# Six of thirty exponentials computed as powers on GpSimd, under another fixed order of all engines

## The chip, the cores and the metric

The kernel runs on one core of one Trainium2 chip. The metric is the device time of one execution in microseconds (us), lower is better. A core has TensorE (matrix products into PSUM, eight banks), VectorE (DVE in the profile), ScalarE (ACT), GpSimd (POOL) and SyncE (SP, which here only issues transfers). Each engine works through its own list of instructions in order; semaphores make it wait for others.

## The reference, cut to what matters

Two branches work on the same `A_x` of 2048 tokens by 640 columns, and a gate per token mixes them. (The second input, `B_x`, isn't used by the result.)

```python
x = A_x
g = sigmoid((x * gate_w).sum(-1, keepdims=True))
return g * A(x, wq, wk, wv, wo, beta) + (1 - g) * B(x, w_r, w_i)

def A(...):                       # 32 heads of 20, four segments of 512 tokens
    phi = lambda t: where(t > 0, t + 1.0, exp(t))
    for s in range(4):
        logits = qs @ ks^T * scale + mask     # causal within the segment
        a_dot = softmax(logits) @ vs
        a_mem = (phi(qs) @ M) / (phi(qs) @ z + 1e-06)
        outs.append(sigmoid(beta) * a_mem + (1 - sigmoid(beta)) * a_dot)
        M = M + phi(ks)^T @ vs
        z = z + phi(ks).sum(tokens)
    return concat(outs) @ wo

def B(x, w_r, w_i):               # 2-D Fourier filter
    return irfft2(rfft2(x) * (w_r + 1j * w_i))
```

`phi` is what the change touches. It is needed for `q` in segments 1 to 3 (the memory is empty in segment 0) and for `k` in segments 0 to 2 (nothing reads the memory after segment 3). Queries and keys of a segment are five tiles of 128 rows (head columns) by 512 tokens, so there are 6 x 5 = 30 tiles.

## The kernel before

The attention branch goes segment by segment. `proj_tile` (L1007) makes one tile of `q` or `k`: matmuls into a PSUM bank, a copy into SBUF (`ev_proj`, on ACT or VectorE), a store to DRAM from where the heads are read back padded (`qkp`), and then `phi` of the tile. `phi` is three instructions: `phi_exp` (L1052, on ACT) writes exp of the tile into one of two buffers `et`; `phi_max` (L1064, VectorE) writes max(t, 0) + 1 into `phq` or `phk`; `phi_min` (L1065, VectorE) takes the minimum of the two. For `k`, a transposing load `pkT` then makes `pkn`, which the memory update multiplies with `va`.

The attention itself takes head groups of four. `qk_unit` makes the logits in four PSUM banks, ACT writes their exponentials into `ex` (L1247), GpSimd zeroes what lies above the diagonal (`mask`, L1273), and `pv_flipped` (`pv_group` in the last segment) multiplies with the values. `ex` has three buffers, so a group's exponentials need the buffer that the third group before it used. `ev_pv` copies the result into `ub`. Beside all this runs the Fourier branch, as matrix products against tables: `fold` sums of rows on VectorE and GpSimd, `F1`, `D`, `T`, then the product with the filter (`W_mul` on VectorE, L1429; `W_add`, L1434, on VectorE or GpSimd), and back (`Tb`, `Db`). `finish_tile` makes the output. Reversed copies of `x` (`xrev`, L924) are made by ACT or GpSimd.

No loop sets the order. The kernel first records all 2291 operations, each with its possible engines, a cost of the planner's and its dependencies. Then `schedule` goes through a list written out in the kernel, `ORDER` (L550): each code is twice the operation's number plus the choice among its engines. Every engine gets its instructions in the order of this list, and `emit` adds the semaphore waits that the dependencies need. A second list, `HOMES` (L538), names the PSUM bank of each result. So an instruction whose input is late holds up all that the list places behind it on its engine.

Costs in the planner are a fixed part and a part per column in nanoseconds. `either` (L493), for a VectorE instruction that GpSimd can do instead, gives GpSimd 120 + 1.95 per column.

Of the kernel before, what the change touches and what calls it, by code (L numbers as in the profile page):

```python
# [417 lines left out]
SC = float(DH) ** -0.5  # L418


class Kern:
# [79 lines left out]
    def dma(self, dst, src, nbytes, r, w, prio, tr=False, name="", after=(), queue="sp"):  # L501
# [343 lines left out]
    def consts(self):  # L845
# [10 lines left out]
        for i in range(2):  # L856
            self.one("pool", lambda e, i=i: e.memset(self.va[i].ap(0, [1, 4 * H * VW + 16]), 1.0), 2816, [],
                     [b("va", i, lt, h) for lt in range(4) for h in range(2)], 0.0)
# [738 lines left out]
```

## Time and profile before

| | |
|---|---|
| three runs | 248.64, 255.21, 257.80 us |
| their median | 255.21 us |
| span of the profiled execution | 246.3 us |
| mean granted TensorE clock | 0.999 |
| instructions | 11384 |

The profile is of one execution: the span goes from its first instruction to its last. What lies around the span isn't part of it; the fastest of the three runs is 2.3 us above it. The page gives each engine's busy time and then the chain of work that ended last; the views of the trace group instructions by line and tile, and give waits as total, times and longest in us. A group's row reads: line, engine, operation, output and input tiles with their shapes, count, then busy us and mean ns of one, then idle us before them and what ended it. L484 and L482 are the PSUM copies of `copy_alts` on VectorE and ACT.

### The profile page before, as it was taken

The numbers are of one execution on the slowest core, as the hardware profiler recorded it, in microseconds if no ns is written. First come the engines' busy times: TensorE is split into PE (matmuls) and PEld (weight loads), VectorE is DVE, ScalarE is ACT, GpSimd is POOL, SyncE is SP. The second block draws the span as 40 slices with busy tenths as digits, with TensorE's granted clock in tenths as the row PEclk, the third lists the DMA queues.
The fourth block names the chain that finished last, engine by engine and source line by source line (L and its number), as shares of the span: only waits on it lengthen the run. The fifth ranks groups of instructions, "written<-read, shape, count | busy, mean of one in ns | idle before, by whom it ended". The sixth has DMA issues, their size and how long they took to land.

```text
span 246.3 us, 11384 instructions
## 1 busy us (share of the span) xinstructions
PE 223.4 (91%) x4926; PEld 145.0 (59%) x4926; DVE 193.4 (79%) x475; ACT 197.5 (80%) x231; POOL 149.9 (61%) x276
## 2 busy tenths in 40 slices
PE   6999998799799899999869997999899889999992
PEld 1576566677466466556635754546555557667891
DVE  0189897689799799799899798999989784755552
ACT  2199977879799899899878987998899959798720
POOL 8123327147656944828966984866887558567810
PEclk9999999999999999999999999999999999999999
DMA  7899779985659495669762783444866567952223
GB/s 170 263 368 189 211 216 182 296 141 164 149 156 243 143 178 153 193 175 187 212 161 65 227 233 73 141 142 157 247 183 150 140 172 181 150 122 72 68 93 96
DMA packets 58933, 42.25 MB, mean 172 GB/s; under 512 B 30020, under 2 KB 55172, under 8 KB 58884
## 3 DMA queue, kind: packets, MB, share of 16 engines
q1 hardware_dynamic: 57188, 40.71, 65.8%
q10 hardware_dynamic: 1696, 0.82, 1.3%
q8 instruction: 39, 0.64, 1.1%
q14 instruction: 10, 0.08, 0.1%
HBM read 23.32 MB, written 12.30 MB: 145 GB/s over the span
## 4 chain that ended last, share of the span: by engine, by line
PE 40%; DVE 15%; DMA 14%; ACT 12%; SPq 8%; POOL 5%; issue 3%; DVEq 0%; ACTq 0%; POOLq 0%
PE psum L473 25%; PE psum L471 15%; ACT ex L1247 11%; SPq L505 5%; SPq L507 4%; POOL ex L1273 4%; DMA fcat<-tab_fcat 3%; DMA tt<-tab_tt 2%; DMA pkn<-phk 2%; DVE Pt L1429 2%; DMA qk_scr<-qu 2%; DMA xsb<-in_A_x_dram 2%; DMA u_scr<-ub 2%; DVE phq L1064 2%; DVE Cp L484 2%
## 5 line engine op out<-in xcount | busy, mean ns | idle before, releaser
L1247 ACT ACTIVATE ex<-psum 128x2048 bf16<-128x2048 f32 (+4 forms) x92 | 137.2, 1505 | 17.6 <-PE psum L473 13.9
L1273 POOL TENSOR_SCALAR_AFFINE_SELECT ex<-ex 128x256 bf16<-128x256 bf16 (+3 forms) x191 | 93.8, 514 | 32.2 <-ACT ex L1247 27.7
L473 PE MATMUL psum<-qkp 20*64 20x64 bf16 (+5 forms) x1024 | 32.1, 266 | 5.7 <-ACT ex L1247 3.0
L1429 DVE TENSOR_TENSOR Pt<-psum,Wt 128x642 bf16<-128x642 f32 x32 | 25.8, 818 | 3.6 <-PE psum L473 2.1
L1434 POOL TENSOR_TENSOR Yt<-Pt 128x321 bf16<-128x321 bf16 x24 | 17.5, 736 | 15.5 <-DVE Pt L1429 11.9
L473 PEld LDWEIGHTS psum<-qkp 20*64 20x64 bf16 (+1 forms) x1024 | 12.4, 100 | 23.9 <-ACT ex L1247 14.1
L473 PE MATMUL psum<-xT,wk 128*128 128x256 bf16 (+1 forms) x220 | 22.4, 293 | 0.8 <-DMA xT<-in_A_x_dram 0.8
L471 PE MATMUL psum<-wo,oU 128*32 128x320 bf16 x480 | 20.4, 299 | 0.8 <-DVE oU L1524 0.8
L877 POOL TENSOR_TENSOR xsb<-xf 128x318 bf16<-128x318 bf16 (+2 forms) x9 | 7.0, 793 | 20.7 <-DVE xf L872 20.7
L473 PEld LDWEIGHTS psum<-xT,wk 128*128 128x128 bf16 (+1 forms) x220 | 14.7, 102 | 6.9 <-issue 3.6
L473 PE MATMUL psum<-ex,va 128*32 128x192 bf16 (+4 forms) x480 | 17.7, 273 | 0.8 <-DVE Cp L484 0.3
L473 PE MATMUL psum<-xT,wq 128*128 128x512 bf16 (+1 forms) x95 | 18.0, 419 | 0.0
L1475 DVE TENSOR_TENSOR G<-eo,psum 128x320 bf16<-128x320 f32 x32 | 14.0, 479 | 4.0 <-PE psum L473 3.5
L1095 DVE TENSOR_TENSOR va<-psum,ebx 128x320 bf16<-128x320 f32 x32 | 15.1, 480 | 1.6 <-ACT gate L1093 0.7
L473 PEld LDWEIGHTS psum<-ex,va 128*32 128x32 bf16 x480 | 11.8, 96 | 7.7 <-issue 1.4
L1052 ACT ACTIVATE et<-qu 128x512 bf16<-128x512 bf16 x25 | 15.6, 628 | 0.2 <-DVE phq L1065 0.2
L473 PE MATMUL psum<-wv,xT 128*128 128x320 bf16 (+2 forms) x90 | 15.3, 248 | 0.0
L471 PEld LDWEIGHTS psum<-wo,oU 128*32 128x32 bf16 x480 | 12.4, 97 | 4.5 <-DVE oU L1524 1.1
L484 DVE CAST Cp<-psum 65x256 bf16<-65x256 f32 (+1 forms) x26 | 13.6, 536 | 1.6 <-PE psum L471 1.2
L484 DVE CAST ot<-psum 128x320 bf16<-128x320 f32 x17 | 8.2, 490 | 7.5 <-PE psum L471 3.5
L872 DVE TENSOR_TENSOR xf<-xsb 128x640 bf16<-128x640 bf16 x16 | 7.3, 482 | 8.1 <-DMA xsb<-in_A_x_dram 8.1
L471 PE MATMUL psum<-xT,wq 128*32 128x512 bf16 x160 | 11.6, 380 | 2.3 <-DVE va L1095 1.3
(122 smaller groups left out, 472.9 us busy)
## 6 DMA issues: line engine op xcount, KB each, us to landing
qkp<-qk_scr SPq DMA_DIRECT2D x28, 160.0 KB
tt<-tab_tt SPq DMA_DIRECT2D x8, 512.0 KB, 5.2
qk_scr<-qu SPq DMA_DIRECT2D x12, 256.0 KB, 3.3
u_scr<-ub SPq DMA_DIRECT2D x12, 256.0 KB, 3.5
xsb<-in_A_x_dram SPq DMA_DIRECT2D x8, 320.0 KB, 6.9
oU<-u_scr SPq DMA_DIRECT2D x15, 128.0 KB, 3.8
out_dram<-ot SPq DMA_DIRECT2D x12, 160.0 KB
Wt<-in_B_w_i_dram SPq DMA_DIRECT2D x16, 80.2 KB, 3.2
```

The costliest lines, as they stand in the source:

```text
L471: h = e.matmul(dst, wt, r_, start=st, stop=sp_, **{**kw, "tile_position": (0, q), "skip_group_check": True})
L473: h = e.matmul(o_, l_, r_, start=st, stop=sp_, **kw)
L484: alts["dve"] = (lambda e: e.tensor_copy(dst(), src()), 67 + 1.04 * n, 68.0)
L505: return e.dma_start_transpose(d_, s_)
L507: return e.dma_start(d_, s_)
L1052: self.one("act", lambda e: e.activation(et.ap(0, [1, L]), qsl(), ACT.Exp), L, [qb], [b("et", pi_)], late, name="phi_exp")
L1095: self.one("dve", lambda e: e.tensor_tensor(va.ap(i * H * VW + h0 * VW, [VW, 16], [1, DH]), self.ps(bank, 0, [DH, 16], [1, DH]), self.ebx. ...
L1247: self.one("act", lambda e, d=d, q=q: e.activation(self.ex.ap(*d), self.ps(bank, *q), ACT.Exp, scale=SC), n, [bank], [self.exb(s, 2 * pr + ...
L1273: self.one("pool", lambda e: e.affine_select(self.ex.ap(e0 + d0, [1280, n4], [1, n], np_=np_), self.ex.ap(e0 + s0, [1280, n4], [1, n], np_ ...
L1429: self.one("dve", lambda e, ri=ri, Pt=Pt, Wt=Wt, wo_=wo_, bank=bank: e.tensor_tensor(Pt.ap(ri * 322, [644, 2], [1, KD]), self.ps(bank, 0, ...
L1434: fn = lambda e, r=r, a0=a0, a1=a1, op=op, Pt=Pt, Yt=Yt: e.tensor_tensor(Yt.ap(r * 322, [1, KD]), Pt.ap(a0 * 322, [1, KD]), Pt.ap(a1 * 322 ...
L1475: self.one("dve", lambda e, q=q, n2=n2, bank=bank, eo=eo: e.tensor_tensor(self.G.ap(n2 * D + 639 * q, [1 - 2 * q, 320]), eo.ap(q, [1, 320] ...
```

## The change

A constant tile `eul` of two float32 numbers e is set by VectorE at the start. `phi_exp` gets a second engine: GpSimd raises e (read with stride 0 over 512 columns) to the power of the tile, in one two-input instruction. The planner's cost for it is the one that `either` has. The two lists are replaced by others; in the new `ORDER` six of the thirty `phi_exp` have the code of GpSimd: segment 1's `q` tiles 1, 2 and 4 and `k` tiles 0 and 3, and segment 3's `q` tile 1. The other entries are the same operations in another order and, for some, on the other of their two engines.

```diff
+EULER = 2.718281828459045
...
     HOMES = (
-        4, 4, 5, 7, 6, 7, 6, 5, 7, 6, 4, 5, 7, 4, 5, 6, 6, 4, 5, 5, 4, 4, 7, 0, 0, 0, 0, 0, 6, 5, 0, 0, 0, 0, 0, 6, 7, 0, 0, 0, 0, 0, 4, 7, 0, 0, 0,
...
+        4, 4, 5, 7, 6, 6, 4, 4, 7, 4, 7, 5, 7, 5, 4, 5, 6, 4, 7, 5, 5, 7, 4, 0, 0, 0, 0, 0, 5, 6, 0, 0, 0, 0, 0, 6, 6, 0, 0, 0, 0, 0, 7, 5, 0, 0, 0, 0, 0, 7,
...
     ORDER = (
-        25, 0, 104, 26, 74, 23, 2, 4, 28, 6, 8, 10, 12, 72, 30, 14, 16, 190, 18, 46, 20, 34, 214, 44, 90, 202, 36, 192, 52, 194, 204, 48, 206, 178,
...
+        4525, 4540, 4542, 4544, 4546,
     )
...
+        self.eul = T("eul", [P, 2], F32)
...
+        self.one("dve", lambda e: e.memset(self.eul.ap(0, [1, 2]), EULER), 2, [], [b("eul")], -2.0, name="eul")
...
-            self.one("act", lambda e: e.activation(et.ap(0, [1, L]), qsl(), ACT.Exp), L, [qb], [b("et", pi_)],
-                     late, name="phi_exp")
+            fexp = lambda e: e.activation(et.ap(0, [1, L]), qsl(), ACT.Exp)
+            fpow = lambda e: e.tensor_tensor(et.ap(0, [1, L]), self.eul.ap(0, [0, L]), qsl(), ALU.pow)
+            self.Sc.op({"act": (fexp, 65 + 0.833 * L, 110.0), "pool": (fpow, 120 + 1.95 * L, 50.0)}, r=[qb, b("eul")], w=[b("et", pi_)], prio=late, name="phi_exp")
```

Counted from the two lists, by engine (before, after):

| operation | ACT | VectorE | GpSimd |
|---|---|---|---|
| `phi_exp` | 30, 24 | | 0, 6 |
| `xrev` | 2, 0 | | 2, 4 |
| `ev_pv` (to `ub`) | 7, 17 | 17, 7 | |
| `ev_proj` | 24, 19 | 15, 20 | |
| `ev_F1`, `ev_D`, `ev_Tb`, `ev_Db` | 38, 34 | 62, 66 | |
| `final` | 15, 11 | 17, 21 | |
| `fold` | | 39, 35 | 12, 16 |
| `W_add` | | 8, 11 | 24, 21 |
| `normal`, `addmem` | | 21, 25 | 10, 6 |

199 rows, old and new, of tables (HOMES, ORDER) are left out of this document.

## The prediction

> **What bounds the kernel now.** I read the page's busy table first, then the chain of work that ended last, then the waits.
>
> ```profile
> span 246.3 us, 11384 instructions
> ...
> PE 223.4 (91%) x4926; PEld 145.0 (59%) x4926; DVE 193.4 (79%) x475; ACT 197.5 (80%) x231; POOL 149.9 (61%) x276
> ...
> PE 40%; DVE 15%; DMA 14%; ACT 12%; SPq 8%; POOL 5%; issue 3%; DVEq 0%; ACTq 0%; POOLq 0%
> ```
>
> The busy table says that TensorE has work in 91% of a span of 246.3 us, and that GpSimd is the one with room: 96.4 us idle. The last row follows the end of the kernel back. TensorE is 40% of it, ACT 12%, GpSimd 5%. So the kernel is a TensorE kernel whose other engines are nearly as full, and each is now and then the one that is waited for.
>
> ```profile
> POOL ex L1273 <- ACT ex L1247: 27.7, 23, 3.9
> ...
> PEld psum L473 <- ACT ex L1247: 14.1, 39, 0.7
> ACT ex L1247 <- PE psum L473: 13.9, 26, 1.5
> ...
> PE psum L473 <- ACT ex L1247: 3.0, 10, 0.5
> ...
> ACT ex L1247 <- POOL ex L1273: 1.8, 3, 0.9
> ...
> PEld psum L473 <- POOL ex L1273: 1.5, 4, 0.6
> ```
>
> These are the waits between the three engines of the attention (total, times, longest). ACT and TensorE wait for each other in small pieces, 14 us one way and 14 + 3 the other: a loop in balance. GpSimd's masks wait for ACT's exponentials (27.7 us), but hardly anybody waits for a mask: 1.8 + 1.5 us in the whole run. The masks are on time because GpSimd is mostly ready when an exponential ends. That is the cover which this change spends.
>
> **What leaves ACT.** Reading the two lists of codes (operation number is code // 2, engine is code % 2) gives the moves: six `phi_exp` go from ACT to GpSimd, both `xrev` copies that ACT had go to GpSimd, and of the PSUM copies ACT, net by kind, gives 17 away and takes 14, ten of these for `ub`.
>
> ```profile
> L1052 ACT ACTIVATE et<-qu x25: 608/626/660, 35.7 to 163.5; 128x512 bf16<-128x512 bf16 x25
> ...
> L924 ACT ACTIVATE xR<-xT 128x1280 bf16<-128x1280 bf16 x2 | 2.6, 1277 | 0.0
> ...
> L482 ACT ACTIVATE ub<-psum 128x512 bf16<-128x512 f32 x7 | 4.2, 595 | 0.4 <-PE psum L473 0.4
> ...
> L482 ACT ACTIVATE ot<-psum 128x320 bf16<-128x320 f32 x15 | 6.3, 440 | 2.9 <-PE psum L473 1.5 <-ACT ot L482 0.5 <-DMA out_dram<-ot 0.4
> ```
>
> Six exponentials at 0.626 us (minimum, median, maximum in the first row) are 3.8 us; two `xrev` at 1.28 are 2.6; three copies at 0.44 to 0.60 are 1.3 to 1.8. ACT is relieved of about 7.9 us of 197.5. On the path ACT holds 12%, so by shares this is worth 1 us; if ACT were the one that is waited for throughout, all 7.9. I take 1 us, since PE's share is larger and PE's own work stays.
>
> **What GpSimd gets besides.** Two `xrev`, net four fold pieces; it gives three `W_add`, two `normal` and two of the `addmem` on `oU` to VectorE.
>
> ```profile
> L924 POOL COPY xR<-xT 128x1280 bf16<-128x1280 bf16 x2 | 2.5, 1242 | 0.0
> ...
> L877 POOL TENSOR_TENSOR xsb<-xf 128x320 bf16<-128x320 bf16 x2 | 1.6, 788 | 2.7 <-DVE xf L872 2.7
> ...
> L1434 POOL TENSOR_TENSOR Yt<-Pt 128x321 bf16<-128x321 bf16 x24 | 17.5, 736 | 15.5 <-DVE Pt L1429 11.9 <-PE psum L471 2.1 <-DVE Cp L484 1.2
> ...
> L1516 POOL TENSOR_TENSOR oU<-oU,r 128x512 bf16<-128x512 bf16 x3 | 3.5, 1152 | 0.4 <-DMA oU<-u_scr 0.4
> ...
> L1524 POOL TENSOR_TENSOR oU<-oU,mT 128x640 bf16<-128x640 bf16 x3 | 4.7, 1576 | 6.1 <-DVE oU L1516 4.2 <-DVE rs L1310 1.9
> ...
> L1516 DVE TENSOR_TENSOR oU<-oU,r 128x512 bf16<-128x512 bf16 x12 | 4.9, 436 | 1.0 <-DMA oU<-u_scr 1.0
> ```
>
> Added: 2 x 1.24 + 4 x 0.79 = 5.6 us. Given away: 3 x 0.74 + 2 x 1.15 + 2 x 1.58 = 7.7. So GpSimd is 2 us better off before the powers are counted. VectorE gets these seven for less (the `normal` costs it 0.436 in place of 1.152), some 3 us, and about as many copies as it loses. I cost this at nothing: it lies in VectorE's 53 us of idle time, and were that gone it would be 3 us. The new constant `eul` is one tiny VectorE memset at the start.
>
> **What a power costs** is the open price; no row shows one. From below: a GpSimd instruction that reads two tensors of 512 columns takes 1.15 us (`oU<-oU,r`), nearly the 1.118 us that the planner's line writes in for the power. From above I use the slope of the simplest GpSimd instruction.
>
> ```profile
> L1273 POOL TENSOR_SCALAR_AFFINE_SELECT ex<-ex 128x256 bf16<-128x256 bf16 x84 | 35.9, 434 | 18.4 <-ACT ex L1247 15.3 <-ACT gate L1093 2.8
> L1273 POOL TENSOR_SCALAR_AFFINE_SELECT ex<-ex 128x512 bf16<-128x512 bf16 x54 | 35.8, 670 | 7.0 <-ACT ex L1247 5.7
> ```
>
> 256 more columns cost 0.236 us here, so one simple step over 512 columns is 0.47. A power with a tensor as exponent is a logarithm, a product and an exponential. If an engine without a table makes them of simple steps, twenty on top of the two-input pass give 1.15 + 20 x 0.47 = 10.6 us; eight give 4.9; none, if all hides under the reads, 1.15. The number of steps is my assumption, and the price an estimate between these rows. I take 4.9: the floor would mean that a power is as cheap as a product, and I hold that for the least likely. ACT's 0.626 for the same 512 exponentials is no guide to another engine.
>
> The Trainium skill (GPSIMD Engine Reference, section 3.1) says that GpSimd runs loops in software, bound by about 3 operations a cycle from three operations per element on; no run here shows that. With 40 operations, an assumed count, an estimate by that page at its 1.2 GHz is 5.7 us, and the sum below would be 5 us more. It is the rule that speaks against this change.
>
> **Where the powers stand.** From the lists: three of segment 1 (`q` tiles 1 and 2, `k` tile 0) stand among GpSimd's work that ran between 36 and 56 us before, two (`k` tile 3, `q` tile 4) among that of 64 to 77, one (segment 3, `q` tile 1) among that of 120 to 134.
>
> ```profile
> core 0: us, POOL busy (x), PEclk, DMA share, GB/s
> 36.00:56.00 20.00, 9.36 (x19) 1.00 0.93 198
> 64.00:77.00 13.00, 6.25 (x15) 1.00 0.78 186
> 120.00:134.00 14.00, 9.75 (x17) 1.00 0.45 123
> ```
>
> GpSimd's idle time there is 10.6 + 6.8 + 4.3 = 21.6 us, or 3.6 us for each of the six. Behind the first power GpSimd has fold pieces (which the spectral half's first matmuls need) and three masks; behind the second and third, masks of the next head groups; behind the fourth and fifth `mask1088`, `mask1152`, `mask1216`, the pieces that a group's value product needs last; behind the sixth two of these. A late mask holds that product, TensorE behind it in its fixed order, the copy of the product on ACT or VectorE, and, since `ex` has three buffers, the exponential that refills it. VectorE also stops at `phi_min`, which now waits for GpSimd, and behind it in its list stand `ev_v`, `W_mul` and `ev_D`, which free PSUM. The powers issue no transfer, but the transposing load `pkT` of the two `k` tiles waits for their `phi_min` on SyncE's queue, and the transfers listed behind it start later by as much.
>
> An idle time only covers what falls into it, and an order in which each mask is placed to be just in time can't move the masks. I count half of it, 10.8 us, as cover; both ends stay for the range (21.6 and none).
>
> **The sum.** 6 x 4.9 = 29.4 us of powers, less 10.8 of cover, is 18.6 of stall; less 1 us for ACT: +17.6. The profiled execution has a span of 246.3 us; the fastest run is 248.64, so 2.3 us lie around it, and 246.3 + 2.3 + 17.6 = 266.2. The three runs shown have a median of 255.21, 6.6 us above that; on it the sum is 272.8. I forecast 268, between the two and nearer to the profile, from which all terms come.
>
> **Rivals.** (1) *The power is as cheap as the plan says*: 6 x 1.15 = 6.9 us fall into 21.6 of idle time and cost nothing, and the relief of ACT counts, 1 to 7.9 us, say 4.5: 248.6 - 4.5 = 244 from the profile, 251 from the median. Faster; it decides below about 1.8 us a power (10.8 / 6). For it speaks GpSimd's 39% idle, against it that a power would have to cost no more than a product. Chance of faster 0.18.
>
> (2) *The power costs 2 to 3.6 us*: 12 to 21.6 us against 10.8 to 21.6 of cover, less ACT's relief: between -2% and +2%, 250 to 258. Chance 0.14. Shifts of the order alone lie in here too: matmuls stand a median of 4 places elsewhere in the list, transfers 3, at most 39, and TensorE's 23 us without work bound what a better order can win.
>
> (3) *Each power also stops VectorE.* The trace has this on a small scale:
>
> ```profile
> L1065 DVE TENSOR_TENSOR phq<-phq,et x15: 360/424/2692, 39.8 to 168.3; 128x512 bf16<-128x512 bf16 x15
> ...
> 146.29 1.41 POOL L1434 TENSOR_TENSOR Yt<-Pt 128x321 bf16<-128x321 bf16 x2
> ...
> 146.39 2.69 DVE L1065 TENSOR_TENSOR phq<-phq,et 128x512 bf16<-128x512 bf16 x1
> ...
> 147.67 0.47 POOL L1351 TENSOR_TENSOR Mz<-Macc,hm 128x154 bf16<-128x154 f32 x1
> 148.10 2.24 POOL L1273 TENSOR_SCALAR_AFFINE_SELECT ex<-ex 128x512 bf16<-128x512 bf16 x4
> ```
>
> A VectorE instruction that takes 0.42 us as a rule took 2.69 while GpSimd ran without a gap beside it. If one of them meets each power, VectorE stands too and nothing covers: 6 x 4.9 - 1 = 28.4, 277 from the profile, 284 from the median. Chance 0.2. The Trainium skill (SBUF — State Buffer, Who interferes with whom) has this as an exclusive lock for the whole instruction between GpSimd and a VectorE instruction with two SBUF inputs; the rows above agree in direction, without showing that it is whole.
>
> (4) *The power takes 10.6 us or more*: 63.6 - 10.8 - 1 = 52, 300 from the profile and 307 from the median; longer still if it goes lane by lane, which nothing here bounds. Chance 0.16.
>
> That leaves 0.32 for the forecast with a price of 3.6 to 8 us, whose own range is 256 to 285. The range for 8 in 10 goes from 246 (within the cheap case) to 305 (within the last). Two per cent is about what a measurement of this kernel, whose three runs spread by 3.6%, can tell. Faster 0.18, within 0.14, slower 0.32 + 0.2 + 0.16 = 0.68.
>
> **What would show it.** A row `POOL TENSOR_TENSOR et<-eul,qu` x6: its mean is the test of all, near 4.9 here, 1.15 in the first rival, over 10 in the last. ACT's busy time near 190, GpSimd's near 148 + 6 x price. The wait of `ex` on ACT for POOL `ex` and of PEld for POOL `ex`, 3.3 us together, should rise to over 10, and a wait of VectorE's `phi_min` for POOL `et` appear. VectorE instructions of several us beside a power would show rival 3. Wrong I am if the power is under 2 us, or if it is long and these waits stay small.

## The result and the profile after

The changed kernel takes 732.24 us, median of 4 runs (731.31 to 733.09); the kernel before, on the same occasions, 251.93, median of 4 (247.04 to 257.8). The ratio is 2.950 [2.934, 2.966]: slower, as forecast, by a size that lies far outside the forecast's 246 to 305. Some executions of a kernel take some per cent longer at a lower granted clock; the ratios, and the medians given from here on, leave those out.

The page of the changed kernel, its span, its busy times and the chain that ended last:

```profile
span 729.5 us, 11709 instructions
...
PE 239.1 (33%) x5098; PEld 149.9 (21%) x5098; DVE 201.2 (28%) x482; ACT 193.3 (26%) x220; POOL 640.9 (88%) x281
...
PE   8910005100010001700003000299700007998898
...
POOL 6499999999999999899999999965899997576743
PEclk9965557655555555755555555599955557999989
...
POOL et L1049 67%; PE psum L474 13%; PE psum L472 7%; ACT ex L1244 2%; DVE G L1472 1%; DMA wk<-in_A_wk_dram 1%; POOL ex L1270 1%; DVE Pt L1426 1%; SPq L506 1%; DVE mem L1141 0%; DVE qu L485 0%; DVE eo L485 0%; DVE Yt L1431 0%; DVE Ac L485 0%; DVE dn L1136 0%
```

GpSimd went from 149.9 us of work to 640.9, and two thirds of the chain is one line, the powers. TensorE's slices are at 0 or 1 in 24 of the 27 in which GpSimd's are at 9. The group of that line among GpSimd's, and the same instructions by tile (minimum, median, maximum):

```profile
L1049 POOL TENSOR_TENSOR et<-eul,qu 128x512 bf16<-128x512 f32 x6 | 491.6, 81936 | 5.5 <-ACT Ac L483 2.8 <-DVE phq L1062 1.4 <-DVE qu L485 1.3
```

```profile
L1048 ACT ACTIVATE et<-qu x19: 620/622/651, 119.0 to 647.2; 128x512 bf16<-128x512 bf16 x19
...
L1049 POOL TENSOR_TENSOR et<-eul,qu x6: 81912/81938/81957, 34.2 to 522.6; 128x512 bf16<-128x512 f32 x6
```

A power of one tile takes 81.94 us, all six within 0.05 us of each other; the exponential of such a tile on ACT takes 0.622. Six powers are 491.6 us, and the span grew by 729.5 - 246.3 = 483.2. The waits show how it comes to the end (total, times, longest):

```profile
ACT ub L483 <- PE psum L474: 162.5, 7, 81.4
...
PEld psum L474 <- POOL ex L1270: 159.4, 7, 79.1
PE psum L474 <- POOL ex L1270: 158.8, 3, 80.4
...
DVE omh L976 <- POOL gg L973: 80.0, 1, 80.0
...
DVE phk L1062 <- POOL et L1049: 78.8, 1, 78.8
...
PEld psum L474 <- POOL xsb L873: 78.2, 1, 78.2
DVE phq L1062 <- POOL et L1049: 77.9, 1, 77.9
PE psum L474 <- POOL xsb L873: 77.8, 1, 77.8
...
DVE gg L972 <- POOL gate L964: 76.9, 1, 76.9
```

Each power stands for a wait of 77 to 81 us. Only two of them are by the one who needs the power itself (`phi_min`, on `phk` and `phq`). The others wait for something small that stands behind it in GpSimd's list: a mask, a fold piece (`xsb`), a gate of four columns. Then the rest stops too: ACT for a product that TensorE can't make.

### The profile page after: what moved, and what is told of

The parts are those of the page before. It is cut to its first block, busy times and chain, and to the rows that moved or that the text cites. A ratio compares the mean times of both kernels' runs of the same rounds, so it can differ in the third digit from the quotient of the medians.

```text
span 729.5 us, 11709 instructions
## 1 busy us (share of the span) xinstructions
PE 239.1 (33%) x5098; PEld 149.9 (21%) x5098; DVE 201.2 (28%) x482; ACT 193.3 (26%) x220; POOL 640.9 (88%) x281
## 4 chain that ended last, share of the span: by engine, by line
POOL 68%; PE 21%; DVE 5%; ACT 2%; issue 1%; SPq 1%; DMA 1%; DVEq 0%; ACTq 0%
POOL et L1049 67%; PE psum L474 13%; PE psum L472 7%; ACT ex L1244 2%; DVE G L1472 1%; DMA wk<-in_A_wk_dram 1%; POOL ex L1270 1%; DVE Pt L1426 1%; SPq L506 1%; DVE mem L1141 0%; DVE qu L485 0%; DVE eo L485 0%; DVE Yt L1431 0%; DVE Ac L485 0%; DVE dn L1136 0%
## 5 line engine op out<-in xcount | busy, mean ns | idle before, releaser
L1049 POOL TENSOR_TENSOR et<-eul,qu 128x512 bf16<-128x512 f32 x6 | 491.6, 81936 | 5.5 <-ACT Ac L483 2.8
L474 PE MATMUL psum<-ex,va 128*32 128x512 bf16 (+4 forms) x480 | 19.0, 291 | 238.3 <-POOL ex L1270 158.6
L474 PE MATMUL psum<-big,Ac 128*128 128x161 bf16 (+2 forms) x60 | 11.7, 282 | 156.4 <-DVE Bt L485 80.4
L483 ACT ACTIVATE ub<-psum 128x512 bf16<-128x512 f32 x17 | 10.2, 597 | 162.7 <-PE psum L474 162.5
L483 ACT ACTIVATE qu<-psum 128x512 bf16<-128x512 f32 x12 | 7.1, 595 | 161.4 <-PE psum L474 160.8
L474 PEld LDWEIGHTS psum<-big,Ac 128*128 128x128 bf16 x60 | 5.4, 105 | 161.1 <-DVE Bt L485 81.3
L474 PE MATMUL psum<-fcat,xsb 128*128 128x128 bf16 x60 | 7.0, 225 | 77.8 <-POOL xsb L873 77.8
L1062 DVE TENSOR_TENSOR phk<-phk,et 128x512 bf16<-128x512 bf16 x15 | 7.5, 505 | 79.0 <-POOL et L1049 78.8
L1062 DVE TENSOR_TENSOR phq<-phq,et 128x512 bf16<-128x512 bf16 x15 | 7.0, 463 | 78.0 <-POOL et L1049 77.9
L483 ACT ACTIVATE Ac<-psum 128x512 bf16<-128x512 f32 x9 | 5.4, 596 | 79.2 <-PE psum L474 79.2
L1431 POOL TENSOR_TENSOR Yt<-Pt 128x321 bf16<-128x321 bf16 x21 | 15.7, 751 | 10.5 <-DVE Pt L1426 6.0
```

What stands on the lines that cost most here:

```text
L474: h = e.matmul(o_, l_, r_, start=st, stop=sp_, **kw)
L483: alts["act"] = (lambda e: e.activation(dst(), src(), ACT.Copy), 65 + 0.833 * n, 110.0)
L1049: fpow = lambda e: e.tensor_tensor(et.ap(0, [1, L]), self.eul.ap(0, [0, L]), qsl(), ALU.pow)
L1062: fmin = lambda e: e.tensor_tensor(dst(), dst(), et.ap(0, [1, L]), ALU.min)
L1431: fn = lambda e, r=r, a0=a0, a1=a1, op=op, Pt=Pt, Yt=Yt: e.tensor_tensor(Yt.ap(r * 322, [1, KD]), Pt.ap(a0 * 322, [1, KD]), Pt.ap(a1 * 322 ...
```

## The experiments

The theory from here: the price of the powers is all; where they stand, the new order and the 8 us taken from ACT count for nothing beside it. Rivals: the new order loses by itself; GpSimd holds VectorE's port; long stops cost more than their own length.

**The new order alone.** In the changed kernel's list the six codes go back to ACT, at the same places (the six codes, wherever they stand in the list):

```diff
-1921, 1943, 1961, 2053, 2071, 3271,
+1920, 1942, 1960, 2052, 2070, 3270,
```

> The changed kernel with its six powers put back on ACT as exponentials, each at the place of the list that its power had: the new order alone. If the price of the powers is all (82 us by six), the whole 483 us go and the time is within 2% of the kernel before, 244 to 258 us, with TensorE's granted clock back from 0.66 to 0.99 or more. If the new order is bad by itself, over 260 us stay; if it is better, as the 8 us taken from ACT would have it with the six still on ACT's list, 240 to 247.

Measured: 250.25 us, median of 6, beside 250.95 of the kernel before (median of 8); ratio 0.996 [0.990, 1.001]. All of the 483 us are gone and TensorE's granted clock in the profiled run is 1.0. The order is neither bad nor a gain that can be told.

> The new order with all thirty exponentials on ACT once more, with more rounds: whether this order is worth taking over without the powers. If the six exponentials on ACT cost the order what the relief would have saved, the ratio is 0.99 to 1.01; if the order is a real gain, under 0.99 with an interval that leaves out 1.

Measured once more: 252.29 us, median of 5, but beside a single run of the kernel before, 249.59, which gives no interval (the medians of all runs are 252.65 and 256.37). Whether this order is worth half a per cent stays open, and no version here is shown to beat the kernel before.

**What the plan thought.** A product in place of the power, so that the instruction has the price of the plan:

```diff
-            fpow = lambda e: e.tensor_tensor(et.ap(0, [1, L]), self.eul.ap(0, [0, L]), qsl(), ALU.pow)
+            fpow = lambda e: e.tensor_tensor(et.ap(0, [1, L]), self.eul.ap(0, [0, L]), qsl(), ALU.mult)
```

> The changed kernel with a product in place of each power (e times t, so phi of six tiles is another function): what the plan thought that a power costs. The row on GpSimd should be 1.15 us by six, as the other two-input instructions of 512 columns. The first rival of the prediction gives 244 us from the profile to 251 from the median; if half of the idle time counts as cover, 6.9 us are hidden and the time is at or 1 to 4 us under that of the order with exponentials on ACT; if nothing is hidden, 7 us over it.

Its row, from the view of the tile `et`:

```profile
L1049 POOL TENSOR_TENSOR et<-eul,qu x6: 1033/1042/1225, 37.7 to 129.9; 128x512 bf16<-128x512 f32 x6
```

1.04 us each, and 250.84 us, median of 6, ratio 0.999 [0.992, 1.005]. So at the plan's price the change would have been no change that can be told. Six times 1.04 on GpSimd is hidden, but the relief of ACT isn't worth anything that shows either: against the order with the exponentials on ACT, which has six of them more on ACT (3.8 us), it is not faster. The two intervals leave room for 1 or 2 us either way. The first rival's gain of 4.5 us was too hopeful by its ACT term.

**The price by columns.** Powers of 16, 30 and 128 columns of each tile; what is left out of `et` keeps its old content, so `phi` of six tiles is partly wrong (the edit for 30; those for 16 and 128 differ in the number alone):

```diff
-            fpow = lambda e: e.tensor_tensor(et.ap(0, [1, L]), self.eul.ap(0, [0, L]), qsl(), ALU.pow)
+            fpow = lambda e: e.tensor_tensor(et.ap(0, [1, 30]), self.eul.ap(0, [0, 30]), qt.ap(qo, [1, 30]), ALU.pow)
```

> The changed kernel with powers of 30 of the 512 columns only (the rest of each buffer keeps what it held). If a power costs by the column, 81.9 / 512 = 0.160 us, each takes 4.8 to 5.0 us, which is the price that the prediction had assumed for the whole. Its sum is tested so: half of GpSimd's idle time as cover gives 18 us over the order with exponentials on ACT; full cover gives 8; no cover 28. If a power has a large fixed part (code that is loaded, say), the row stays far over 5 us.

> The changed kernel with powers of 16 of the 512 columns (the rest of each buffer keeps what it held): 0.344 + 16 x 0.1594 = 2.89 us each by the line through the 30 and the 512 columns, 17.4 us by six. With the cover of 10.8 us that the prediction had taken it is 6.6 us over the order with exponentials on ACT (256 to 258 us); with the 15 us that the powers of 30 columns found, 2 over (251 to 254); if the cover grows with the price, below 1.

> The changed kernel with powers of 128 of the 512 columns: 20.7 us each, 124.4 by six. With 15 us of cover, as for 30 columns, it is 109 over the order with exponentials on ACT: 358 to 362 us. If the long stops cost something beyond their own length (TensorE's granted clock falls in them and comes back late), 5 to 10 us more; if more is covered the longer the stop, less than 355.

The rows of the three, from the same view:

```profile
L1049 POOL TENSOR_TENSOR et<-eul,qu x6: 5097/5125/5142, 34.5 to 137.5; 128x30 bf16<-128x30 f32 x6
```

```profile
L1049 POOL TENSOR_TENSOR et<-eul,qu x6: 2892/2919/3014, 35.3 to 128.8; 128x16 bf16<-128x16 f32 x6
```

```profile
L1049 POOL TENSOR_TENSOR et<-eul,qu x6: 20712/20738/20756, 36.1 to 217.7; 128x128 bf16<-128x128 f32 x6
```

The price is a straight line: (81.94 - 5.125) / (512 - 30) = 0.1594 us a column and 0.34 fixed; 16 and 128 columns lie on it within 0.03 us. This makes it a scale of prices to try the prediction's sum on. The time over the order with exponentials on ACT (250.25), and what is hidden of the six:

| columns | one power, us | six | time, us | over 250.25 | hidden |
|---|---|---|---|---|---|
| 16 | 2.92 | 17.5 | 256.25 | 6.0 | 11.5 |
| 30 | 5.13 | 30.8 | 266.08 | 15.8 | 14.9 |
| 128 | 20.74 | 124.4 | 363.87 | 113.6 | 10.8 |
| 512 | 81.94 | 491.6 | 732.24 | 482.0 | 9.6 |

Some 10 to 15 us are hidden, whatever the price: about half of the 21.6 us of GpSimd's idle time, or somewhat more. The rows are of three occasions and medians of the kernel before lie between 247.8 and 251.5 on them, so a difference of 3 or 4 us between two rows of the last column says little; taken over the kernel before of the same occasion, the column reads 12.7, 15.7, 12.0 and 7.2. The expectation for 16 columns with a cover of 10.8 (256 to 258) is met; the one for 128 (358 to 362) is missed by 2 us, which is within that difference. At 30 columns, with about the price that the prediction had assumed for the whole power, the time is 266.08, ratio 1.059 [1.052, 1.065]. At 16 the ratio is 1.025 [1.010, 1.040]. So the price from which a loss shows lies between 1.04 and 2.9 us.

In the kernel with powers of 30 columns the waits for masks that the prediction had named are there, where the page before has 1.5 us and the order with exponentials 1.8:

```profile
PEld psum L474 <- POOL ex L1270: 7.2, 8, 3.1
PE psum L474 <- POOL ex L1270: 6.4, 3, 3.6
```

**One power in the old order.** The kernel before with one code changed (and `eul` set beside the first memset):

```diff
-3268,
+3269,
```

> The kernel before, with its own order, and one power (segment 3, q tile 1) on GpSimd at the place in the list where ACT had the exponential. If each power costs its full price on the path whatever the order, the time is 78 to 82 us over the kernel before, 325 to 335 us. If the damage comes from the new order around the powers, less than 60 over. If GpSimd holds VectorE by a lock for the whole power, a VectorE instruction with two inputs in SBUF shows tens of us; if not, none is over 3 us.

Measured: 332.52 us in one run, 81.6 over the 250.95 of the kernel before beside it, for one power of 81.96. Its longest waits:

```profile
PEld psum L474 <- POOL ex L1276: 80.4, 6, 78.7
DVE ub L485 <- PE psum L474: 80.1, 3, 79.2
ACT qu L483 <- POOL et L1055: 78.9, 1, 78.9
PE psum L474 <- POOL ex L1276: 78.7, 2, 78.6
```

TensorE waits for a mask behind the power, VectorE for TensorE, and ACT for the power itself, whose input `qu` it is to overwrite. So the order around the powers isn't the cause: a power costs about its length in the old order as in the new one.

**The price by itself.** A small kernel with one instruction after the other (`tt` is GpSimd's `tensor_tensor`, `x` 512 columns of the input in bfloat16, `xf` and `pos` their exponentials in float32 and bfloat16, `eub` the constant in bfloat16):

```python
...
run(tt(ap(o["p1"], L, 1), ap(eul, L, 1, 0), ap(x, L, 1), ALU.pow))         # then 8, 16 and 64 rows
run(tt(ap(o["half"], L // 2), ap(eul, L // 2, step=0), ap(x, L // 2), ALU.pow))
run(tt(ap(o["zero"], L), ap(eul, L, step=0), ap(zero, L), ALU.pow))        # exponents all zero
run(tt(ap(o["bb"], L), ap(eub, L, step=0), ap(x, L), ALU.pow))
run(tt(ap(o["ff"], L), ap(eul, L, step=0), ap(xf, L), ALU.pow))
run(tt(ap(o["pow"], L), ap(eul, L, step=0), ap(x, L), ALU.pow))            # VectorE beside this one
run(tt(ap(o["big"], L), ap(pos, L), ap(x, L), ALU.pow))
```

> A kernel of its own that computes nothing of the reference (its output is a copy of the first input): powers of several shapes and operands on GpSimd one after another, a product of 512 columns beside them, and three VectorE instructions while a power of 128x512 runs. If a power goes through a core's lanes one after another, it takes time by the rows of 16: 82 us at 16, 64 and 128 partitions, 41 at 8, about 5 at 1. If it goes by columns whatever the lanes, all five take 82 us. If the price hangs on the values, the power with exponent zero is far under 82; if on the types, those with float32 exponent or bfloat16 base differ. 256 columns: 41 us if it goes by the column. If GpSimd holds the port for the whole power, VectorE's two-input product, its max-and-add and its sum take tens of us; if not, under 1 us each.

Its timeline (start, duration, what):

```profile
5.18 1.04 POOL L67 TENSOR_TENSOR o_mult<-eul,x 128x512 bf16<-128x512 f32 x1 [4.74 <-DVE zero L91]
6.30 81.91 POOL L68 TENSOR_TENSOR o_p<-eul,x 1x512 bf16<-1x512 f32 x1
88.29 81.91 POOL L69 TENSOR_TENSOR o_p<-eul,x 8x512 bf16<-8x512 f32 x1
...
252.26 81.92 POOL L71 TENSOR_TENSOR o_p<-eul,x 64x512 bf16<-64x512 f32 x1
334.25 41.12 POOL L72 TENSOR_TENSOR o_half<-eul,x 128x256 bf16<-128x256 f32 x1
375.45 81.92 POOL L73 TENSOR_TENSOR o_zero<-eul,zero 128x512 bf16<-128x512 f32 x1
457.45 81.92 POOL L74 TENSOR_TENSOR o_bb<-eub,x 128x512 bf16<-128x512 bf16 x1
539.45 81.92 POOL L75 TENSOR_TENSOR o_ff<-eul,xf 128x512 bf16<-128x512 f32 x1
621.44 81.92 POOL L76 TENSOR_TENSOR o_pow<-eul,x 128x512 bf16<-128x512 f32 x1
621.47 1.29 DVE L94 TENSOR_TENSOR o_v_mult<-pos,x 128x512 bf16<-128x512 bf16 x1 [616.46 <-POOL o_ff L75]
622.79 0.29 DVE L95 TENSOR_SCALAR o_v_lock<-x 128x512 bf16<-128x512 bf16 x1
623.12 0.43 DVE L96 TENSOR_TENSOR o_v_lock<-pos,x 128x512 bf16<-128x512 bf16 x1
703.44 82.03 POOL L77 TENSOR_TENSOR o_big<-pos,x 128x512 bf16<-128x512 bf16 x1
```

Of what was varied, nothing but the number of columns moves the price. One row costs as much as 128, an exponent of zero as much as a real one, and neither type nor base makes 0.2 us. A power is 79 times the product of the same operands (81.92 / 1.04). A power doesn't go through the rows one after another, or 8 rows would cost half of 16.

The last rows are on the port. VectorE's product of two SBUF tiles began 0.03 us after the power and took 1.29 us; its two successors took 0.29 and 0.43, the usual time, while the power ran on for 79 us. So VectorE lost less than 0.9 us at the power's start, and not the power's length. The kernel with one power in the old order shows the same, with a VectorE instruction of one input that takes 0.286 us as a rule (the median of `phq<-qu` there) and began 0.01 us after the power:

```profile
127.36 81.96 POOL L1055 TENSOR_TENSOR et<-eul,qu 128x512 bf16<-128x512 f32 x1
127.37 1.18 DVE L1067 TENSOR_SCALAR phq<-qu 128x512 bf16<-128x512 bf16 x1
```

It too was 0.9 us longer, and no later VectorE instruction beside that power took more than 0.81. In the changed kernel VectorE's instructions with two inputs in SBUF, which began 1.3 us or more behind the start of the first power, took their usual time:

```profile
34.24 81.96 POOL L1049 TENSOR_TENSOR et<-eul,qu 128x512 bf16<-128x512 f32 x1 [2.85 <-ACT Ac L483]
...
35.60 0.42 DVE L1062 TENSOR_TENSOR phk<-phk,et 128x512 bf16<-128x512 bf16 x1
35.93 0.49 DVE L868 TENSOR_TENSOR xf<-xsb 128x640 bf16<-128x640 bf16 x1
...
37.18 0.33 DVE L873 TENSOR_TENSOR xsb<-xf 128x320 bf16<-128x320 bf16 x1
```

## Why the prediction was right in its way and wrong in its size

**What failed** is one term: "I take 4.9". The price was 81.94, 17 times that, and nearly 8 times the upper bound of 10.6 from twenty simple steps. The sum took the price from no row: the bound was built from the slope of GpSimd's masks and a number of steps that I had assumed; no row of the profile before stood anywhere near a power, and the text said so, but the range treated the assumed twenty as an end. With the measured price the prediction's own sum gives 491.6 - 10.8 - 1 = 479.8 over 248.6, that is 728.4, beside the measured 731.31 to 733.09.

**The cover**, half of GpSimd's idle time around the powers (10.8 us), was about right: 10 to 15 us by the table of columns. That it is half was a choice between none and all, which no row had given, so its fitting is in part luck. The kernel with powers of 5.13 us takes 266.08, near the 266.2 that the sum gives from the profile for a power of 4.9. That they agree to a tenth is luck: with 5.13 the sum is 248.6 + 30.8 - 10.8 - 1 = 267.6.

**The relief of ACT** was taken as 1 us and is worth nothing that can be told, by the kernel with products. The durations of ACT's instructions add up to some 7.5 us less than before, about as said, but its busy time, in which what overlaps counts once, fell by only 4.2, to 193.3 and not to "near 190". No work that TensorE has to do became less.

**GpSimd's other moves and VectorE's**, costed at nothing, cost nothing that shows: the order alone is 0.996 [0.990, 1.001], though VectorE's busy time rose by 7.2 us in it (193.4 to 200.6) and not by the 3 that had been named.

**The ways in which it was to show** are there but for two: the row on `et`, GpSimd's busy time (640.9, by "148 + 6 x price" 639.6), TensorE's waits for masks, and `phi_min`'s wait for `et`. ACT's busy time is one of the two. The other is ACT's own wait for a mask (`ex` for POOL `ex`, 1.8 us before), which is in no view of the changed kernel: ACT waited for TensorE instead, above all for the products that go to `ub`. The mechanism that the prediction named, work queued behind the power on GpSimd rather than the power's own reader, is what most of the long waits are.

**The rivals.** The first (a power as cheap as a product) has the wrong price, and would not have been faster had it been right. The second's mechanism can be seen at 16 columns, 2.92 us: a ratio of 1.025 [1.010, 1.040], just over the 2% that it had named, with the interval on both sides of it. The third (VectorE stopped for the whole power) is refuted by all three timelines. By the page's rule (the Trainium skill, SBUF — State Buffer, Who interferes with whom) the 0.42 us instruction of the changed kernel would have taken some 80 us; the measurement decides, and in the two cases that show a delay it was under 0.9 us. What had held VectorE for 2.69 us in the kernel before, with several short GpSimd instructions beside it, wasn't tried by itself. The fourth (10.6 us or more) was the right direction, with its lane by lane refuted by the one row.

The Trainium skill's 3 operations a cycle (GPSIMD Engine Reference, section 3.1) had given an estimate of 5.7 us with an assumed 40 operations. At that page's 1.2 GHz (section 1) the measured 0.1594 us a column is 191 cycles, an estimate that would stand for some 570 operations at its rate; no run here shows what GpSimd does in them.

**What stays open** is how much of the time the stops cost beyond their length. TensorE's matmuls took 239.1 us of busy time; in the same order with exponentials the page reads:

```profile
PE 224.1 (91%) x5098; PEld 143.6 (58%) x5098; DVE 200.6 (82%) x482; ACT 194.9 (79%) x226; POOL 150.2 (61%) x275
```

The number of matmuls is the same, so 15 us went into their pace. The granted clock in the stretches of the powers is low, as the view by stretches shows (the first power and the fourth, then all behind the last):

```profile
34.20:123.50 89.30, 11.45 (x231) 7.51 (x230) 8.41 (x20) 8.96 (x14) 87.78 (x10) 0.56 0.22 44
...
303.00:386.70 83.70, 5.36 (x93) 2.55 (x84) 4.34 (x15) 3.39 (x3) 83.64 (x4) 0.51 0.05 15
...
604.60:729.50 124.90, 113.03 (x2646) 72.49 (x2646) 94.11 (x221) 92.66 (x102) 75.25 (x141) 0.94 0.55 137
```

(PE, PEld, DVE, ACT and POOL busy, then the clock, the share of the DMA engines and GB/s.) Most of that low clock falls on time in which TensorE has no work. The first of these stretches, cut finer, shows what is left of it for the work:

```profile
34.20:39.20 5.00, 4.95 (x48) 3.02 (x46) 3.93 (x11) 4.18 (x8) 4.96 (x1) 1.00 0.99 171
39.20:116.20 77.00, 0.00 (x0) 0.00 (x0) 0.00 (x0) 0.54 (x1) 77.00 (x2) 0.52 0.13 33
116.20:120.00 3.80, 3.00 (x34) 1.63 (x38) 1.24 (x3) 1.33 (x4) 3.73 (x6) 0.50 0.00 0
120.00:123.50 3.50, 3.50 (x161) 2.86 (x150) 3.24 (x7) 2.91 (x3) 2.09 (x4) 0.99 1.33 158
```

Behind the power, which ends at 116.2 us, TensorE worked for 3.0 us at a clock of 0.50 before it was back at 0.99. How much of the 15 us came onto the path isn't shown. If all of them had, the hidden part would have fallen by as much with the price; from 30 to 512 columns it fell by 5.3, not much more than the 3.6 by which the occasions differ.

## What to carry to other kernels

Before an operation is moved to another engine, measure that operation there, in the shape it will have: an engine may offer it at 79 times the price of its neighbour in the same instruction. Where no row stands near a new price, an upper bound made of assumed steps is no bound, and the range should say so by its width. An engine's idle time covers a longer instruction only in part (here about half of what stood idle nearby), since the engine's other work has its place in the order and is waited for.

## What the runs showed of the hardware that I had not expected

A power on GpSimd costs 0.1594 us a column plus 0.34, and depended neither on rows (1 to 128) nor on the values and types tried. Two VectorE instructions, one with one input and one with two in SBUF, that began within 0.03 us of a power's start took up to 0.9 us longer than usual; those that began later beside the same powers didn't. TensorE's granted clock, 1.0 in the same order without powers, was 0.52 while TensorE stood behind the first power and 0.50 in the first 3.8 us after it, and the busy time of the same matmuls over the whole run rose by 15 us.
